# A scan followed by a mixture of adapters: stores of four chunks, ScalarE copies as words, and a new static order

## The chip, the cores and the metric

The kernel runs on one core of one Trainium2 chip. The metric is the device time of one execution in microseconds (us), the median of several runs; lower is better.

## What is computed

```
a, b: (8, 6400, 128) float32
h = 0;  for t in range(6400):  h = a[:, t] * h + b[:, t];  x[:, t] = h     # per batch and channel
x = x.reshape(51200, 128)
logits = x @ w_gate                         # (51200, 8)
w = softmax over the two largest logits of each row
delta = sum over the two chosen experts e of  w_e * ((x @ A[e]) @ B[e])   # rank 16
out = x + delta                             # (51200, 128) float32
```

The inputs a and b are 26.2 MB each and the output is 26.2 MB, so some 78.6 MB pass between HBM and the core.

## The kernel before

The 51,200 rows are cut into 100 **chunks** of 512 rows, and a chunk into four **blocks** of 128. Each step of a chunk is an operation with a name, and a table `ORDER` lists, for each of the five instruction queues (`pe` TensorE, `act` ScalarE, `dve` VectorE, `pool` GpSimd, `sp` SyncE), in which order that queue issues its operations. The table is fixed in the source. What an operation waits for is worked out from its dependences and turned into semaphore waits; a queue that waits holds everything behind it.

The steps, with their names in `ORDER` and their lines:

- `la`, `lb` (L396, SP): load a and b. From chunk 4 on one transfer brings two chunks (512 KB) in rows of 4 KB; the first four chunks come singly in rows of 2 KB. There are `NL` = 6 buffers each for a and b, and a load waits until TensorE has read the pair that was in its buffer six pairs earlier.
- `A`, `B`, `P` (L417, TensorE): turn a and b to channels by rows in PSUM, by transposes. `P17` holds b of chunk 17 and a of chunk 18.
- `ae` (L435, ScalarE): copy a from PSUM to SBUF. `fi` (L446, TensorE): `FILL` transposes of the identity matrix into pA ahead of chunks 7 to 14, whose results are not used.
- `sc` (L482, VectorE): the scan along the rows, into xT, float16, a ring of `NX` chunks.
- `Z` (L500, TensorE): logits and x @ A for a unit of mostly six blocks; `ze` (L506, ScalarE) copies them to zl, a ring of `NZ` blocks.
- `g1` to `g8`, `gx` (L534 to L554, VectorE and GpSimd) and `w1` (L549, ScalarE): the gate weights of a group of units, mostly 24 blocks.
- `mu` (L569, GpSimd or VectorE): multiply by the gate weights into zw.
- `T` (L578, TensorE): transpose zw into PSUM, float16. `te` (L300, ScalarE or VectorE): copy it to zwT in SBUF.
- `D` (L588, L589, TensorE): x by the identity plus zwT @ B. `oe` (L300, ScalarE or VectorE): copy the result to outt, a ring of `NO` blocks.
- `st` (L631, SP): store one entry of `STORES`, in chunks. With two chunks each partition holds eight rows of the output side by side, so the transfer has rows of 4 KB; with one chunk, 2 KB.

Which row of the output lies in which partition follows from the store that a chunk belongs to (`tile_of`). `xblock` picks the rows of a block with that stride, so the logits of any block of a store wait for the scans of all its chunks (`zlogits`, `fronts`). `SPLIT` sends the store of chunk 68 as two transfers of 124 and 4 partitions. The last twelve chunks (`TAIL_CHUNKS`) also use the PSUM banks of pA and pB for their results.

Which engine does `te`, `oe`, `mu` and most gating steps follows from the list of `ORDER` in which the name stands.

Of the kernel before, what the change touches and what calls it, by code (L numbers as in the profile page):

```python
# [12 lines left out]
STORES = [2] * 48 + [1] * 4  # L13
SPLIT = {68: [124, 4]}
TOP8 = 4
WARM = 16
FILL = {k: 4 for k in range(7, 15)}
# [3 lines left out]
NX = 24  # L21
NZ = 120
NO = 72
NW = 4
NG = 8
NS = 16
TAIL_CHUNKS = 12
ORDER = {
# [16 lines left out]
    ),  # L45
    "act": (
# [16 lines left out]
    ),  # L63
    "dve": (
# [14 lines left out]
    ),  # L79
    "pool": (  # L80
# [8 lines left out]
    ),  # L89
# [641 lines left out]
```

## Time and profile before

| What | Value |
|---|---|
| Median of 3 runs | 201.59 us (201.13 to 202.28) |
| Profiled execution | 201.01 us, span 199.2 us |
| TensorE, ScalarE, VectorE, GpSimd busy | 93%, 89%, 88%, 68% of the span |
| Mean rate of the DMA engines | 398 GB/s, 22,921 packets |
| Granted TensorE clock | 0.994 |
| Stores | 53 transfers: 47 of 512 KB, 4 of 256 KB, one of 496 KB and one of 16 KB |

The span runs from the first to the last instruction of the profiled execution; the rest of its time lies around it. A share of busy time is a mean over the whole span, with filling and emptying in it. A DMA share in the views adds up the recorded times of packets on 16 engines; packets of one engine overlap a little in the records, so a full stretch shows slightly over 1.

### The profile page before, as it was taken

The page shows a single profiled execution, that of the slowest core. Times are in us where ns is not written, and L with a number is a line of the kernel's source. Part 1 is how long each engine was busy: PE and PEld are TensorE (multiplying, and loading weights), DVE is VectorE, ACT ScalarE, POOL GpSimd, SP SyncE. Part 2 cuts the span into 40 slices and gives each one's busy share as a digit, 9 for nine tenths or more (in the row PEclk, how much of TensorE's full clock was granted, in tenths as well). Part 3 has the DMA queues.
Part 4 walks back from the last instruction along what each step waited for, and adds up shares of the span by engine and source line. Part 5 has one row for each costly group of instructions (what it writes and reads, how often), then busy time and mean ns, then how long its engine had stood idle before and what let it go on. Part 6 is the DMA issues. An engine that isn't in the chain of part 4 may idle for free.

```text
span 199.2 us, 7709 instructions
## 1 busy us (share of the span) xinstructions
PE 185.2 (93%) x3224; PEld 165.5 (83%) x3224; DVE 175.0 (88%) x291; ACT 176.9 (89%) x327; POOL 136.0 (68%) x168
## 2 busy tenths in 40 slices
PE   6899999999998979999999999999999999999990
PEld 6778888889987968899989989889988978878970
DVE  1599999989999879799999999999999899899980
ACT  2378699999988979899999999999999989999981
POOL 3210186878786657969989998796598978676520
PEclk9999999999999999999999999999999999999997
DMA  5999999999999999999999999999999999999796
GB/s 214 385 414 406 410 407 407 409 406 410 411 410 413 414 411 412 415 414 408 414 415 406 411 410 416 411 411 415 414 412 414 417 410 412 406 393 392 298 405 254
DMA packets 22921, 79.26 MB, mean 398 GB/s; under 512 B 2664, under 2 KB 2920, under 8 KB 22888
## 3 DMA queue, kind: packets, MB, share of 16 engines
q1 hardware_dynamic: 22312, 78.39, 98.1%
q8 instruction: 25, 0.41, 0.8%
q10 hardware_dynamic: 576, 0.40, 0.6%
q14 instruction: 8, 0.07, 0.1%
HBM read 52.56 MB, written 26.21 MB: 395 GB/s over the span
## 4 chain that ended last, share of the span: by engine, by line
PE 80%; ACT 5%; DMA 4%; issue 3%; SPq 2%; POOL 2%; DVE 1%; DVEq 0%
PE pB L417 23%; PE pO L588 13%; PE pZ L500 13%; PE pO L578 12%; PE pO L589 10%; PE pA L417 5%; DMA a_tm<-in_a_dram 4%; ACT outt L300 3%; PE pA L446 2%; SPq L396 2%; POOL zw L569 2%; ACT zwT L300 1%; ACT a_st L435 1%; ACT zl L506 1%; DVE xT L482 1%
## 5 line engine op out<-in xcount | busy, mean ns | idle before, releaser
L482 DVE TENSOR_TENSOR_SCAN xT<-a_st,xT,pB 128x512 f16<-128x512 f32 x96 | 120.4, 1254 | 6.6 <-PE pA L417 3.1
L569 POOL TENSOR_TENSOR zw<-zl,g 128x512 f16<-128x512 f32 x90 | 94.5, 1065 | 29.2 <-DVE g L554 23.2
L417 PE MATMUL pB<-ident_f,b_tm 64*128 64x64 f32 (+1 forms) x784 | 67.5, 229 | 1.2 <-issue 0.5
L417 PE MATMUL pA<-ident_f,a_tm 64*128 64x64 f32 (+1 forms) x784 | 67.8, 229 | 0.6 <-issue 0.4
L435 ACT COPY a_st<-pA 128x512 f32<-128x512 f32 x100 | 59.0, 613 | 7.9 <-PE pA L417 7.2
L417 PEld LDWEIGHTS pB<-ident_f,b_tm 64*128 64x128 f32 (+1 forms) x784 | 55.8, 139 | 10.9 <-issue 3.4
L506 ACT COPY zl<-pZ 128x816 f32<-128x816 f32 (+1 forms) x69 | 58.1, 842 | 1.7 <-PE pZ L500 1.6
L588 PE MATMUL pO<-ident_h,xT 128*128 128x128 f16 x368 | 55.2, 233 | 2.0 <-issue 1.8
L417 PEld LDWEIGHTS pA<-ident_f,a_tm 64*128 64x128 f32 (+1 forms) x784 | 56.0, 139 | 1.2 <-DMA a_tm<-in_a_dram 0.7
L300 ACT COPY outt<-pO 128x512 f32<-128x512 f32 x87 | 52.2, 609 | 4.6 <-PE pO L589 4.1
L589 PE MATMUL pO<-cst_h,zwT 128*128 128x128 f16 x368 | 53.0, 219 | 1.7 <-issue 1.7
L588 PEld LDWEIGHTS pO<-ident_h,xT 128*128 128x128 f16 x368 | 46.3, 144 | 4.9 <-issue 2.1
L589 PEld LDWEIGHTS pO<-cst_h,zwT 128*128 128x128 f16 x368 | 39.6, 108 | 1.8 <-issue 1.8
L500 PE MATMUL pZ<-cst_h,xT 128*128 128x136 f16 x400 | 37.8, 229 | 0.5 <-issue 0.4
L578 PE MATMUL pO<-ident_h,zw 128*128 128x128 f16 x368 | 35.5, 220 | 1.1 <-POOL zw L569 0.4
L500 PEld LDWEIGHTS pZ<-cst_h,xT 128*128 128x128 f16 x400 | 30.6, 145 | 1.5 <-DVE cst_h L324 0.2
L578 PEld LDWEIGHTS pO<-ident_h,zw 128*128 128x128 f16 x368 | 22.3, 97 | 5.5 <-POOL zw L569 1.3
L300 DVE COPY zwT<-pO 128x512 f16<-128x512 f16 x56 | 23.0, 414 | 3.5 <-PE pO L578 3.1
L300 ACT COPY zwT<-pO 128x512 f16<-128x512 f16 x36 | 21.4, 600 | 0.9 <-PE pO L578 0.8
L545 POOL TENSOR_TENSOR L<-L,k 128x192 f32<-128x192 f32 x14 | 8.8, 631 | 4.6 <-DVE L L543 4.0
L482 DVE TENSOR_TENSOR_SCAN xT<-a_st,pB 128x512 f16<-128x512 f32 (+1 forms) x8 | 7.5, 938 | 4.5 <-PE pB L417 4.4
L548 POOL TENSOR_TENSOR k<-k,L 128x192 f32<-128x192 f32 (+1 forms) x17 | 9.1, 535 | 2.5 <-DVE L L539 1.8
(56 smaller groups left out, 120.0 us busy)
## 6 DMA issues: line engine op xcount, KB each, us to landing
a_tm<-in_a_dram SPq DMA_DIRECT2D x48, 512.0 KB, 13.3
b_tm<-in_b_dram SPq DMA_DIRECT2D x48, 512.0 KB, 13.4
out_dram<-outt SPq DMA_DIRECT2D x47, 512.0 KB, 11.9
a_tm<-in_a_dram SPq DMA_DIRECT2D x4, 256.0 KB, 4.9
out_dram<-outt SPq DMA_DIRECT2D x4, 256.0 KB, 4.0
b_tm<-in_b_dram SPq DMA_DIRECT2D x3, 256.0 KB, 5.6
out_dram<-outt SPq DMA_DIRECT2D x1, 496.0 KB
b_tm<-in_b_dram ACTq DMA_DIRECT2D x1, 256.0 KB, 4.0
```

Of the source, the lines that this page charges most:

```text
L300: return e.copy(dst, src) if e is eng["act"] else e.tensor_copy(dst, src)
L417: last = e.transpose(*args)
L435: lambda e: e.copy(a_st[c % NA][:, :], pA[:, c % 2, :]))
L482: last = e.tensor_tensor_scan(out=x[:, s0:s1], data0=a_st[c % NA][:, s0:s1], data1=pB[:, c % 2, s0:s1], initial=init, op0=ALU.mult, op1=AL ...
L500: last = e.matmul(pZ[:, k // (n // 2), o : o + W], xblock(b0 + k), Awg_h)
L506: lambda e: e.copy(zl[:, zb : zb + n, :].rearrange("p (h k) w -> p h (k w)", h=2), pZ[:, :, 0 : n // 2 * W]))
L545: d3 = wide(5, [d3], lambda e: e.tensor_tensor(out=ll, in0=ll, in1=kk, op=ALU.add))
L548: d6 = wide(7, [d2, d5], lambda e: e.tensor_tensor(out=kk, in0=kk, in1=ll, op=ALU.add))
L569: lambda e: e.tensor_tensor(out=wv, in0=zv, in1=gv, op=ALU.mult))
L578: last = e.transpose(ptile[:, k * 128 : k * 128 + 128], zz[:, k, :], ident_h[:, :])
L588: e.matmul(dst, xblock(b0 + k), ident_h[:, :], start=True, stop=False)
L589: last = e.matmul(dst, zt[:, k * 128 : k * 128 + 128], B_h, start=False, stop=True)
```

## The change

- `STORES`: 22 stores of four chunks, four of two and four of one, where there were 48 of two and four of one. With four chunks a partition holds sixteen rows of the output side by side, so such a transfer has 1 MB in rows of 8 KB.
- `te` on ScalarE: the same bytes are copied as 256 float32 words instead of 512 float16 elements. On VectorE it stays as it was.
- `FILL`: two transposes instead of four ahead of each of the chunks 7 to 14.
- Rings: xT from 24 to 32 chunks, outt from 72 to 96 blocks, zl from 120 to 80 blocks.
- `ORDER`: all five lists are new, and with them the engine of some operations. ScalarE has 68 `te` and 83 `oe` (before 38 and 95), VectorE 32 `te`, 17 `oe` and 13 `mu` (before 62, 5 and 10).
- `AHEAD`, `TREE` and `MASK` are added with values for which they do nothing: an added dependence between operations of SP that lie 1000 apart (the list has 133), and another form of the last gating step for the groups in `MASK`, which is empty.

```diff
-STORES = [2] * 48 + [1] * 4
-SPLIT = {68: [124, 4]}
+STORES = [2,2]+[4]*16+[2,2]+[4]*6+[1]*4
+SPLIT = {68:[124,4]}
...
-FILL = {k: 4 for k in range(7, 15)}
+FILL = {k:2 for k in range(7,15)}
...
-NX = 24
-NZ = 120
-NO = 72
+NX = 32
+NZ = 80
+NO = 96
...
+AHEAD = 1000
+TREE = ()
+MASK = ()
...
+        for before, op in zip(self.order["sp"], self.order["sp"][AHEAD:]):
+            op.deps = op.deps + [before]
...
-            o_te[c] = P.add("dve act", f"te{c}", J, [o_T[c]] + get(o_D, c - NW),
-                            lambda e: copy(e, zt, ptile[:, 0:C]))
+            o_te[c] = P.add("dve act", f"te{c}", J // 2, [o_T[c]] + get(o_D, c - NW),
+                            lambda e: e.copy(zt.bitcast(F32), bank[:, 0 : C // 2]) if e is eng["act"]
+                            else e.tensor_copy(zt, ptile[:, 0:C]))
```

The lists of SP from the last loads on, before and after:

```diff
-la96 st58 lb96 st60 la98 st62 st72 st64 lb98 st66 st68 st78 st76 st70 st74 st82 st80 st86 st84 st90 st88 st92 st94 st96 st97 st98 st99
+la96 lb96 la98 st56 st60 lb98 st68 st70 st64 st72 st76 st80 st84 st88 st92 st96 st97 st99 st98
```

More of the change, by code (lines that the diff above doesn't have):

```diff
@@ L552, in gating @@
                     zlast[zpos[u] + k] = d5 if top else d2
-            o_g[gi] = wide(8, [a1, d5] + (get(o_mu, glast[gi - NG]) if gi >= NG else []),
-                           lambda e: e.scalar_tensor_tensor(
-                               out=gg, in0=ll, scalar=0.0, in1=sg, op0=ALU.is_ge, op1=ALU.mult))
+            free = get(o_mu, glast[gi - NG]) if gi >= NG else []
+            if gi in MASK:
+                d8 = wide(9, [d5, d6], lambda e: e.tensor_scalar(
+                    out=ll, in0=ll, scalar1=0.0, scalar2=1.0, op0=ALU.is_ge, op1=ALU.mult))
+                o_g[gi] = P.add("pool dve", f"gf_{gi}", nb, [a1, d8] + free,
+                                lambda e: e.tensor_tensor(out=gg, in0=ll, in1=sg, op=ALU.mult))
+            else:
+                o_g[gi] = wide(8, [a1, d5] + free, lambda e: e.scalar_tensor_tensor(
+                    out=gg, in0=ll, scalar=0.0, in1=sg, op0=ALU.is_ge, op1=ALU.mult))
         def back(gi, c):
```

121 rows, old and new, of the table ORDER are left out of this document.

## The prediction

> **What bounds the kernel now.** I read the page first: the five engines' shares, then the forty slices, then the DMA queues.
>
> ```profile
> span 199.2 us, 7709 instructions
> ...
> PE 185.2 (93%) x3224; PEld 165.5 (83%) x3224; DVE 175.0 (88%) x291; ACT 176.9 (89%) x327; POOL 136.0 (68%) x168
> ...
> DMA  5999999999999999999999999999999999999796
> GB/s 214 385 414 406 410 407 407 409 406 410 411 410 413 414 411 412 415 414 408 414 415 406 411 410 416 411 411 415 414 412 414 417 410 412 406 393 392 298 405 254
> ...
> q1 hardware_dynamic: 22312, 78.39, 98.1%
> q8 instruction: 25, 0.41, 0.8%
> ```
>
> Four engines stand near 90%, so the shares alone name no bound. The slices do: the DMA engines move 406 to 417 GB/s from the third slice to the thirty-fourth, flat, whatever the engines do. The profiled execution took 201.01 us with this span of 199.2, so 1.8 us lie around the span; the median of the runs, 201.59 us, is 0.58 above it.
>
> The windows view tests this. Its columns are busy time of PE, PEld, DVE, ACT, POOL (with instructions), granted clock, DMA share, GB/s.
>
> ```profile
> 70.00:80.00 10.00, 8.25 (x151) 7.29 (x148) 8.45 (x13) 8.60 (x17) 6.57 (x9) 1.00 1.02 411
> 100.00:110.00 10.00, 10.00 (x196) 9.26 (x197) 9.82 (x15) 9.98 (x19) 9.15 (x12) 1.00 1.03 412
> 175.00:185.00 10.00, 9.80 (x155) 8.42 (x152) 9.91 (x27) 9.70 (x21) 6.39 (x8) 1.00 0.98 390
> 185.00:195.00 10.00, 8.90 (x136) 7.80 (x133) 8.10 (x37) 9.14 (x21) 3.54 (x5) 1.00 0.90 357
> 195.00:199.20 4.20, 0.00 (x0) 0.00 (x0) 0.00 (x0) 0.00 (x0) 0.00 (x0) 0.73 0.60 230
> ```
>
> PE falls to 8.25 of 10 in one stretch and is full in another, and the DMA rate is 411 and 412. So the bytes set the pace until about 175 us; only in the last 24 us does the share drop, to 0.98, 0.90 and 0.60, where 1.03 is full. The chain of waits gives PE 80%, but PE is followed there through its own queue; how long a transfer waits tells more. The DMA view for 30 to 160 us (columns: count, size, median us from issue to landing), and the queue's own waits:
>
> ```profile
> DMA packets 14631, 53.56 MB, mean 412 GB/s; under 512 B 1620, under 2 KB 1620, under 8 KB 14606
> ...
> b_tm<-in_b_dram SPq DMA_DIRECT2D x38, 512.0 KB, 13.6
> a_tm<-in_a_dram SPq DMA_DIRECT2D x37, 512.0 KB, 13.7
> out_dram<-outt SPq DMA_DIRECT2D x32, 512.0 KB, 14.7
> ```
>
> ```profile
> SPq L396 <- PE pA L417: 36.1, 26, 4.3
> SPq L631 <- ACT outt L300: 23.3, 13, 5.0
> ...
> SPq L631 <- ACT sd L549: 12.9, 4, 8.8
> ```
>
> A load lands 13.6 us after its issue, while 512 KB at 412 GB/s take 1.27 us: ten or eleven transfers stand in line. SP does wait for free buffers (36.1 us in 26 waits, 4.3 at most) and for outputs (8.8 at most), but each wait is shorter than the line, so it never runs empty. A faster engine alone buys nothing here; fewer or cheaper packets do.
>
> **The change part by part.**
>
> *Rows of 8 KB.* 22 stores of four chunks replace 44 of two: 22 x 1 MB in 8 KB rows are 2816 packets where 5632 of 4 KB were, and 52 stores become 30. Bytes stay. What a packet costs beside its bytes is read from packets of two sizes. Stretches of 2 KB rows are the last stores, the head's loads, and a wider stretch of the head that has 4 KB rows and tiny constants in it:
>
> ```profile
> DMA packets 316, 0.59 MB, mean 391 GB/s; under 512 B 32, under 2 KB 32, under 8 KB 316
> ...
> q1 hardware_dynamic: 316, 0.59, 102.2%
> ```
>
> ```profile
> DMA packets 216, 0.40 MB, mean 395 GB/s; under 512 B 26, under 2 KB 26, under 8 KB 216
> ```
>
> ```profile
> 5.00:10.00 5.00, 4.50 (x37) 3.84 (x36) 2.62 (x3) 1.78 (x4) 1.10 (x1) 1.00 1.05 384
> ```
>
> The first is 195.5 to 197 us (single-chunk stores), the second 7 to 8 us. At 391 GB/s over 16 engines a 2 KB packet takes 16 x 2048 / 391 = 83.8 ns, at 412 a 4 KB packet 159.1 ns. Two kilobytes more cost 75.3 ns, so 8.5 ns belong to the packet, its part of the completion write included (8 data packets and one such write per engine and transfer at either size, and with 8 KB rows still). An 8 KB packet then takes 309.7 ns where two of 4 KB take 318.2: 2816 x 8.5 / 16 = 1,496 ns, **1.5 us**. With 395 the packet's part is 6.8 ns and the gain 1.2 us; with 384, 11.6 ns and 2.0 us. I take 391 because those are stores, and alone on the queue.
>
> The other bound lies above nothing: the 16 KB packets of queue 8 took 0.8% of 16 x 199.2 us, 25.5 us for 25, or 1.02 us each, 62 ns per KB where 4 KB packets take 39. [...] For the range I let this term lie between 0 and -2.0 us; a loss as large as queue 8's rate (510 ns per 8 KB, +34 us) I leave out, because the length would then come from size alone, and from 2 to 4 KB the cost per byte falls.
>
> [...]
>
> *The copies of zwT.* On ScalarE a copy of 512 f16 elements becomes one of 256 f32 words.
>
> ```profile
> L300 ACT COPY zwT<-pO 128x512 f16<-128x512 f16 x36 | 21.4, 600 | 0.9 <-PE pO L578 0.8
> L300 ACT COPY outt<-pO 128x512 f32<-128x512 f32 x87 | 52.2, 609 | 4.6 <-PE pO L589 4.1
> L357 ACT CAST cst_h<-pZ 128x128 f16<-128x128 f32 x1 | 0.3, 265 | 0.3 <-PE pZ L351 0.3
> L300 DVE COPY zwT<-pO 128x512 f16<-128x512 f16 x56 | 23.0, 414 | 3.5 <-PE pO L578 3.1
> L300 DVE COPY outt<-pO 128x512 f32<-128x512 f32 x5 | 3.4, 674 | 0.5 <-PE pO L589 0.5
> L569 DVE TENSOR_TENSOR zw<-zl,g 128x512 f16<-128x512 f32 x10 | 6.8, 684 | 0.0
> ```
>
> f16 and f32 of one count take the same 600 and 609 ns, so elements count. Between 128 elements (265) and 512 (609), 256 give about 380 ns. The new order has 68 such copies on ScalarE (38 before) and 83 output copies (95 before): 68 x 0.38 - 38 x 0.60 - 12 x 0.609 = -4.3 us. VectorE gives up 30 copies of zwT, takes 12 output copies and three multiplications: -30 x 0.414 + 12 x 0.674 + 3 x 0.684 = -2.3 us, and five more gating steps of some 0.25 us take back about one. GpSimd loses what these take over. Under the full line that is worth 0 until 175 us. It counts after: behind the copy of chunk 98's a, ScalarE has 11 output copies and 10 of zwT where it had 18 and 7, that is 11 x 0.609 + 10 x 0.38 = 10.5 us for 15.2.
>
> *Fillers.* Sixteen transposes go, at 0.11 us each by the chain's rows:
>
> ```profile
> 16.82 0.44 PE pA L446 x4
> ```
>
> That is 1.8 us of PE between 14 and 26 us. Loads queue there too, so I cost it at nothing; if that cover were missing it would gain, at most 1.8.
>
> *Places and orders.* A block of a four-chunk tile needs all four scans before its logits, two chunks (3.8 us at 1.9 us a chunk) later than now. Cover: the new order of PE runs the transposes of the loads 21 chunks ahead of those of zw around chunk 49, for 18 before; xT has 32 chunks for 24 and outt 24 for 18, but zl only 80 blocks for 120. A store of four waits for four output copies, and the loads behind it on SP wait as well: that is the rival below. Before the last load of b, 64 chunks are stored instead of 68, so 36 are left for the end, not 32. This and ScalarE's 4.7 us give the last stretch more to send: in 185 to 195 the share of 0.90 leaves (1.03 - 0.90) / 1.03 x 10 = 1.3 us unused. I take **0.5 us** of it, the range being 0 to 1.3, because the last stores still wait for the last chunks' scans, gating and copies.
>
> Sum: 199.2 - 1.5 - 0.5 = 197.2 span, 199.0 for the profiled execution, and with the 0.58 above it **199.6 us** as median, 1.0% less. What this kernel's measurement can tell from no change is about 0.5%, 1.0 us.
>
> **The rivals.**
>
> *The rows bring little* (0.13). Rows of 8 KB may go out as packets of 4 KB, or the cost per packet may grow with the row, and the end stays bound by the last chunks. The four-chunk order then trades equal things: 201.6 with nothing saved, 201.0 with half of the 1.2 us; both within 0.5%. For it: no 8 KB packet of queue 1 in the trace. Against it: the cost per packet in two stretches, 6.8 and 8.5 ns. [...]
>
> *SP's line runs dry* (0.19, the slower side). A store of four at SP's head waits for its fourth output copy, and no load behind it goes out. The longest such wait is 8.8 us; doubled, as four chunks double it, it is 17.6 us, against 13.6 us of line. The DMA engines then stand for 4.0 us per such wait. One of them: 201.59 - 1.5 + 4.0 = 204.1; two short ones of 2 us the same. It decides from the point where a store's wait exceeds 13.6 us, in the stretch from 30 us on. For it: the stores' waits in the two rows above come to 36 us already (23.3 + 12.9). Against it: only 4 of those 17 waits are behind gating, the longest of the others is 5.0 us, and stores of 1 MB also lengthen the line.
>
> *More than the sum* (0.06). The dearer packet (2.0 us) and the full 1.3 us of the end: 201.59 - 3.3 = 198.3; with the fillers' 1.8 it would be 196.5.
>
> **How the numbers follow.** The forecast has 0.62; its own range is 198.6 to 200.5. Faster by over 0.5%: 0.62 + 0.06 = 0.68, less 0.01 for its edge, 0.67. Same: 0.13 and that edge, 0.14. Slower: 0.19. The range goes from 198.0, past the third rival's middle, to 202.9, which takes in the second rival where the line is dry for under 2.8 us; left out are the rest of that (0.1) and the far end of the third and others (some 0.08).
>
> **What would show it.** In the new profile the DMA view should have about 2,800 fewer packets of 4 KB and 30 stores, 22 of 1024 KB; between 30 and 160 us the rate should rise from 412 to about 416 GB/s (a third of the bytes at 423), with the share still 1.02 to 1.03. ScalarE's zwT copy should read 128x256 f32 and about 380 ns. The last two windows should show more than 0.90 and 0.60. It is wrong if the rate stays at 412, or if slices in the middle show DMA below 9 and SP's waits at the store line reach 13 us.

## The result and the profile after

The changed kernel takes 203.7 us (median of 4 runs, 202.82 to 204.59) where the kernel before takes 201.49 (median of 4, one more than the three behind the 201.59 above): a ratio of 1.0114, 95% interval 1.0082 to 1.0145. It is 1.1% slower. The forecast was 199.6 us and faster, the range ended at 202.9.

The profiled execution took 204.59 us, the longest of the four. Its page, in the lines that answer to those shown of before:

```profile
span 202.8 us, 7647 instructions
...
PE 188.6 (93%) x3208; PEld 166.8 (82%) x3208; DVE 175.8 (87%) x282; ACT 173.2 (85%) x345; POOL 127.7 (63%) x159
...
GB/s 217 371 419 409 406 406 408 399 383 415 380 414 402 362 415 415 414 356 376 356 417 410 398 422 409 417 407 415 409 417 408 420 415 423 417 409 388 280 346 288
DMA packets 19753, 79.26 MB, mean 391 GB/s; under 512 B 2312, under 2 KB 2568, under 8 KB 16904
...
L593 ACT COPY zwT<-pO 128x256 f32<-128x256 f32 x62 | 23.6, 392 | 3.4 <-PE pO L588 2.3
```

Everything that the change set out to make smaller is smaller. There are 3,168 fewer packets: the 2,816 of the forecast, and 22 fewer transfers with 16 packets under 512 B each (2,312 of these on the page, 2,664 before). In the trace the 2,816 packets of 8 KB take 309 ns each (median; estimate 309.7), those of 4 KB 159 and those of 2 KB 84. The copy of zwT takes 392 ns (estimate 380, before 600). ScalarE is busy 3.7 us less. The span is 3.6 us longer all the same. What is new in the slices is their middle: before, the rate was flat; now it falls to 362, 356 and 376. The windows view of the changed kernel (columns as in the prediction) shows where:

```profile
90.00:100.00 10.00, 9.56 (x186) 8.69 (x184) 9.02 (x12) 9.51 (x20) 8.46 (x11) 1.00 0.98 345
150.00:175.00 25.00, 24.87 (x452) 22.15 (x451) 22.83 (x33) 23.04 (x48) 20.59 (x25) 1.00 1.02 416
175.00:185.00 10.00, 9.72 (x144) 8.25 (x143) 9.52 (x27) 9.29 (x19) 6.53 (x8) 1.00 1.00 412
185.00:195.00 10.00, 9.60 (x156) 8.69 (x153) 9.75 (x34) 9.61 (x28) 5.64 (x8) 1.00 0.71 293
```

Where the transfers run undisturbed (150 to 175 us) the rate is 416 GB/s, the figure that was forecast for 30 to 160 us. From 90 to 100 us it is 345 with a share of 0.98: by their records the DMA engines hardly stood, their packets took longer (those of 4 KB 185 ns in the mean, 162 in the kernel before), and no run shows why. In the last full stretch the share is 0.71, where it was 0.90 before and more than that was forecast, while TensorE is busy for 9.60 of 10 us (8.90 before), VectorE for 9.75 (8.10) and ScalarE for 9.61 (9.14). So at the end it is the computation that is late. The DMA view from 30 to 160 us, and the waits of SP's queue over the whole span:

```profile
DMA packets 12566, 52.18 MB, mean 401 GB/s; under 512 B 1391, under 2 KB 1391, under 8 KB 11039
...
out_dram<-outt SPq DMA_DIRECT2D x15, 1024.0 KB, 16.1
```

```profile
SPq L400 <- PE pA L421: 63.7, 33, 7.2
...
SPq L642 <- ACT outt L304: 18.0, 9, 4.9
...
SPq L642 <- ACT sd L553: 5.6, 1, 5.6
```

The mean rate is 401, not the 416 forecast. The waits at the store line are 5.6 us at most. What grew is the wait of loads for free buffers, 63.7 us in 33 waits where it was 36.1 in 26: the loads wait for TensorE to have read. TensorE's lag is there already after 30 us. The same window of the kernel before and of the changed kernel, and the first scan in each:

```profile
0.00:30.00 30.00, 27.42 (x366) 23.68 (x366) 22.22 (x37) 19.27 (x35) 8.70 (x18) 1.00 0.95 372
...
6.60 1.22 DVE L482 TENSOR_TENSOR_SCAN xT<-a_st,pB 128x512 f16<-128x512 f32 x1 [4.39 <-PE pB L417]
```

```profile
0.00:30.00 30.00, 25.91 (x318) 21.86 (x320) 20.04 (x33) 16.80 (x32) 8.04 (x18) 1.00 0.96 371
...
9.92 1.22 DVE L486 TENSOR_TENSOR_SCAN xT<-a_st,pB 128x512 f16<-128x512 f32 x1 [7.72 <-ACT a_st L439]
```

By 30 us TensorE has begun 48 multiplications fewer, 16 of them fillers, and the first scan starts 3.3 us later.

### The profile page after: what moved, and what is told of

Same layout as the page of the kernel before. It is cut to its first block, busy times and chain, and to the rows that moved or that the text cites. A ratio compares the mean times of both kernels' runs of the same rounds, so it can differ in the third digit from the quotient of the medians.

```text
span 202.8 us, 7647 instructions
## 1 busy us (share of the span) xinstructions
PE 188.6 (93%) x3208; PEld 166.8 (82%) x3208; DVE 175.8 (87%) x282; ACT 173.2 (85%) x345; POOL 127.7 (63%) x159
## 2 busy tenths in 40 slices
DMA packets 19753, 79.26 MB, mean 391 GB/s; under 512 B 2312, under 2 KB 2568, under 8 KB 16904
## 4 chain that ended last, share of the span: by engine, by line
PE 64%; DVE 17%; ACT 6%; POOL 4%; issue 4%; DMA 2%; SPq 0%; DVEq 0%; POOLq 0%
PE pB L421 20%; PE pZ L504 11%; PE pO L599 10%; DVE xT L486 10%; PE pO L588 9%; PE pO L600 7%; PE pA L421 5%; POOL zw L579 4%; DVE zw L579 3%; DMA a_tm<-in_a_dram 2%; ACT zl L510 2%; ACT outt L304 2%; ACT a_st L439 2%; DVE g L564 1%; ACT zwT L593 1%
## 5 line engine op out<-in xcount | busy, mean ns | idle before, releaser
L579 POOL TENSOR_TENSOR zw<-zl,g 128x512 f16<-128x512 f32 x87 | 90.8, 1063 | 22.5 <-DVE g L564 18.1
L421 PE MATMUL pA<-ident_f,a_tm 64*128 64x64 f32 (+1 forms) x784 | 70.2, 231 | 2.1 <-issue 1.3
L421 PE MATMUL pB<-ident_f,b_tm 64*128 64x64 f32 (+1 forms) x784 | 69.9, 231 | 1.9 <-DVE cst_h L328 0.6
L421 PEld LDWEIGHTS pB<-ident_f,b_tm 64*128 64x128 f32 (+1 forms) x784 | 57.1, 140 | 11.9 <-issue 4.4
L304 ACT COPY outt<-pO 128x512 f32<-128x512 f32 x76 | 45.3, 607 | 4.3 <-PE pO L600 3.0
L588 PE MATMUL pO<-ident_h,zw 128*128 128x128 f16 x368 | 34.2, 220 | 1.2 <-issue 0.5
L593 ACT COPY zwT<-pO 128x256 f32<-128x256 f32 x62 | 23.6, 392 | 3.4 <-PE pO L588 2.3
L552 POOL TENSOR_TENSOR k<-k,L 128x192 f32<-128x192 f32 (+2 forms) x16 | 8.6, 535 | 17.1 <-DVE k L542 11.0
L594 DVE COPY zwT<-pO 128x512 f16<-128x512 f16 x30 | 12.3, 411 | 2.7 <-PE pO L588 2.5
L304 DVE COPY outt<-pO 128x512 f32<-128x512 f32 x16 | 10.9, 680 | 1.3 <-PE pO L600 1.2
```

The costliest lines, as they stand in the source:

```text
L304: return e.copy(dst, src) if e is eng["act"] else e.tensor_copy(dst, src)
L421: last = e.transpose(*args)
L579: lambda e: e.tensor_tensor(out=wv, in0=zv, in1=gv, op=ALU.mult))
L588: last = e.transpose(ptile[:, k * 128 : k * 128 + 128], zz[:, k, :], ident_h[:, :])
L593: lambda e: e.copy(zt.bitcast(F32), bank[:, 0 : C // 2]) if e is eng["act"]
L594: else e.tensor_copy(zt, ptile[:, 0:C]))
```

## The experiments

All ratios are to the kernel before, with the 95% interval; the changed kernel itself stands at 1.0114.

**Is the row size worth anything? (rows of 4 KB in the changed kernel)**

```diff
+                if m == 4:
+                    return [e.dma_start(dst[:, h : h + 8], view[:, h : h + 8]) for h in (0, 8)]
...
-                       sem=dma_sem(f"st{len(o_st) % NS}"), parts=len(cuts))
+                       sem=dma_sem(f"st{len(o_st) % NS}"), parts=2 if m == 4 else len(cuts))
```

> The changed kernel, but each store of four chunks goes out as two transfers of 4 KB rows at the same place of the order; nothing else differs. Theory O (the 8 KB rows gain about 1.5 us as predicted, and the new order loses more than that in the middle and at the end): slower than the changed kernel by 0.5 to 1.5 us, 204.2 to 205.2 us. Rival R (8 KB rows or transfers of 1 MB are themselves what costs): faster than the changed kernel, back towards 201.5 us.

Measured: 1.0132 (1.0074 to 1.019). The intervals lie over each other: the 8 KB rows are worth no time that can be measured here, and rival R's return towards 201.5 us did not come. From 150 to 175 us, where the changed kernel has 416 GB/s, this one has 414:

```profile
150.00:175.00 25.00, 24.84 (x451) 22.13 (x448) 22.80 (x33) 22.99 (x49) 20.57 (x25) 1.00 1.03 414
```

**Is the sagging middle the loss? (stores of chunks 8 to 28 moved on SP)**

```diff
-la40 lb40 lb44 la42 la46 lb42 la44 lb48 st8 lb46 la48 st12 la50 la52 lb50 lb52 la54 lb54 la56 lb56 lb58 lb60 la60 la58 la62 lb62 lb64 st20 st16 la64 st24 la66 la68 lb66 lb68 la70 st28
+la40 lb40 st8 lb44 la42 la46 lb42 la44 st12 lb48 lb46 la48 la50 la52 st16 lb50 lb52 la54 lb54 la56 lb56 st20 lb58 st24 lb60 la60 la58 la62 lb62 st28 lb64 la64 la66 la68 lb66 lb68 la70
```

> The changed kernel, but on SP the stores of chunks 8, 12, 16, 20, 24 and 28 stand where the profile shows their outputs ready (the store of chunk 16 was ready at 72.4 us and issued at 97.2), ahead of loads that wait for buffers. Theory O with the loss in the middle (SP's line runs dry because ready stores stand behind waiting loads): the rate between 30 and 160 us rises from 401 to at least 410 GB/s and the time falls by 1 to 3 us, 200.7 to 202.7. Rival E (the end alone decides, since the last chunks are computed too late): the rate rises, the time stays within 0.5 us of 203.7. Rival R: neither changes.

Measured: 1.0201 (1.0145 to 1.0257). The DMA view from 30 to 160 us, a wait of TensorE's weight loads between 100 and 110 us, and two windows right behind it:

```profile
DMA packets 12788, 53.27 MB, mean 410 GB/s; under 512 B 1414, under 2 KB 1414, under 8 KB 11194
```

```profile
PEld pB L421 <- DMA a_tm<-in_a_dram: 3.0, 1, 3.0
```

```profile
104.00:106.00 2.00, 1.24 (x24) 1.24 (x26) 0.08 (x1) 0.08 (x1) 1.55 (x2) 0.55 1.03 424
106.00:108.00 2.00, 2.00 (x30) 1.78 (x30) 1.89 (x3) 1.59 (x4) 0.00 (x0) 0.59 1.01 414
```

The rate rose from 401 to 410, and the time with it, which none of the theories had: the stores now stand ahead of loads on SP, TensorE stood 3.0 us for one load, and behind that its granted clock was 0.55 and 0.59 for some 4 us. A higher DMA rate in the middle does not by itself bring the end forward. Whether the sagging rate costs the changed kernel time stays open, as the moved stores brought this stall with them.

**Is it the last chunks? (chunks 98 and 99 ahead of the backlog)**

```diff
-... Z64 T82 T83 D82 D83 Z65 T84 B99 T85 D84 D85 T86 P98 T87 D86 D87 T91 Z66 T90 T88 T89 D91 Z67 ...
+... Z64 P98 B99 T82 T83 D82 D83 Z65 T84 Z66 T85 D84 D85 T86 Z67 T87 D86 D87 T91 Z68 T90 T88 T89 D91 ...
```

(with the scans and copies of these chunks moved up on VectorE and ScalarE)

> The changed kernel with the last chunks' steps moved ahead of the backlog: on TensorE the transposes of chunk 98's b and 99's a, then of 99's b, right behind the logits of unit 64 (they stood at 184.8 us, 6.0 us after the load of b landed), the logits of units 66 to 68 further up, and the copies, scans and unit copies that belong to them likewise. Theory T: 1 to 4 us faster, 199.7 to 202.7. Rival H: within 0.6 us of 203.7, since the same backlog is only worked off later. Nothing else differs.

Measured: 1.0278 (1.0228 to 1.0328), slower than the changed kernel by some 3 us, where theory T said 1 to 4 us faster and rival H no difference. The theory of the tail fell in this form. That what is moved ahead holds back what it passes is a likely reason, not a shown one.

**Words and fillers alone (kernel before)**

```diff
-FILL = {k: 4 for k in range(7, 15)}
+FILL = {k: 2 for k in range(7, 15)}
...
-                            lambda e: copy(e, zt, ptile[:, 0:C]))
+                            lambda e: e.copy(zt.bitcast(F32), bank[:, 0 : C // 2]) if e is eng["act"]
+                            else e.tensor_copy(zt, ptile[:, 0:C]))
```

> The kernel before with ScalarE's copies of zwT as words and fillers of two instead of four; orders and stores as before. Theory O: within 0.7 us of the kernel before, 200.8 to 202.2, as nothing of it lies on the transfers' path. Rival W (fewer fillers or the word copies slow the head or TensorE): 202.5 us or more.

Measured: 0.9986 (0.9952 to 1.002). Each copy on ScalarE falls from 600 to 384 ns, ScalarE is busy 171.7 us instead of 176.9, and the time stays, as theory O had it.

**Four-chunk stores alone (kernel before)**

```diff
-STORES = [2] * 48 + [1] * 4
+STORES = [2, 2] + [4] * 16 + [2, 2] + [4] * 6 + [1] * 4
...
-NZ = 120
-NO = 72
+NZ = 96
+NO = 96
```

(and the five orders of before, shifted only as far as the wait for four scans asks)

> The kernel before with the stores of the change (22 of four chunks, 8 KB rows) and outt of 96 and zl of 96 blocks; its own orders, in which an operation moves only as far as the wait for four scans asks (some logits by 0.8 to 2.6 us), and each store of four at the place of the later of its two halves. Theory O: the rows gain what was predicted, 0.5 to 1.5 us, so 200.0 to 201.0 us. Rival R: slower than the kernel before by 1 to 3 us, 202.5 to 204.5.

Measured: 1.0655 (1.0599 to 1.0712), 215.25 us, far outside both forecasts. Waits between 30 and 170 us, and a window:

```profile
ACT zl L505 <- PE pZ L499: 11.0, 17, 1.3
DVE zwT L299 <- PE pO L577: 6.3, 13, 1.1
...
PEld pZ L499 <- DVE xT L481: 4.1, 10, 1.1
PEld pZ L499 <- ACT zl L505: 4.0, 8, 1.1
```

```profile
180.00:185.00 5.00, 4.59 (x89) 3.94 (x87) 3.74 (x6) 4.24 (x10) 3.14 (x3) 1.00 0.35 138
```

The logits now wait for scans (`PEld pZ <- DVE xT`), their copies for the logits; in the same stretch of the kernel before the waits of PEld for these do not occur, and that of ScalarE is this:

```profile
ACT zl L506 <- PE pZ L500: 0.4, 1, 0.4
```

At 180 us the DMA engines are a third busy: the backlog of compute ends the kernel.

**The rings as a control (kernel before)**

```diff
-NZ = 120
-NO = 72
+NZ = 96
+NO = 96
```

> The kernel before with zl of 96 and outt of 96 blocks (120 and 72), all else as it was: the control for the rings in the run with stores of four on the orders of before. Theory G (the wait for four scans made that run 14 us slower): within 1 us of 201.5. Rival Z (the smaller ring of zl did): 4 us slower or more.

Measured: 1.0001 (0.9982 to 1.0021). These rings cost nothing. The change's own rings (zl of 80 blocks, xT of 32 chunks) were not run apart.

**Four-chunk stores without the wait for four scans (kernel before)**

```diff
+            def xpair(b):
+                c = b // J
+                s0, n = (c // 2 * 2, 2) if c < NCH - 4 else (c, 1)
...
-            c1 = sum(tile_of[(b0 + n - 1) // J]) - 1
+            c1 = (b0 + n - 1) // J
+            c1 = c1 | 1 if c1 < NCH - 4 else c1
...
-                    last = e.matmul(pZ[:, k // (n // 2), o : o + W], xblock(b0 + k), Awg_h)
+                    last = e.matmul(pZ[:, k // (n // 2), o : o + W], xpair(b0 + k), Awg_h)
...
-            o_D[c] = P.add("pe", f"D{c}", J, [o_te[c]], delta)
+            o_D[c] = P.add("pe", f"D{c}", J, [o_te[c], o_sc[sum(tile_of[c]) - 1]], delta)
```

(with the stores, the rings and the list of SP of the run with four-chunk stores; the last step `D` still waits for all four scans)

> The orders of before, rings of 96 and 96 blocks, stores of four chunks in 8 KB rows, but the logits take their rows as if the store were a pair, and so wait for two scans instead of four (the gate weights and zw then belong to other rows: that part of the computation is changed). Theory G (the wait for four scans is what the stores of four cost): 200 to 202.5 us, near the kernel before, for 215.3 with the wait. Rival S (transfers of 1 MB, sent when the fourth chunk is done, cost by themselves): 208 us or more.

Measured: 1.0038 (1.0013 to 1.0062), 202.12 us. The wait of the logits' copies is back at that of before, in the same stretch:

```profile
ACT zl L512 <- PE pZ L506: 0.4, 1, 0.4
```

So of the 13.8 us between 201.43 and 215.25, 13.1 belong to the wait for four scans and the shifted orders that it asks for. The stores of 1 MB in rows of 8 KB, without that wait, cost 0.7 us and gain nothing.

**Undo the grouping on the new orders (changed kernel, pairs at the places of the fours)**

```diff
-STORES = [2,2]+[4]*16+[2,2]+[4]*6+[1]*4
+STORES = [2] * 48 + [1] * 4
...
-st20 st16 la64 st24
+st20 st22 st16 st18 la64 st24 st26
```

> The changed kernel with stores of two chunks as before (48 pairs and four singles, 4 KB rows), each former store of four as two pairs at its place; its orders and rings otherwise as they are, so that logits wait for two scans again where four were asked. Theory G (the wait for four scans costs in the changed orders): 1 to 3 us faster, 200.7 to 202.7. Rival Q (the orders on the engines cost, wherever the waits are): within 0.7 us of 203.7, as each engine still issues in the same order.

Measured: 1.0187 (1.0143 to 1.0231), if anything slower than the changed kernel, so neither forecast came. Taking the grouping away does not win the time back. That the price now lies in the orders that were drawn for it fits this, but no run shows it by itself.

**What bounds the kernel before? Transfers, TensorE, both ways**

Less to transfer (stores of chunks 8 to 27 write 16 of 128 partitions, some 11 us of transfers), in the kernel before:

```diff
-            cuts = SPLIT.get(c, [128])
+            cuts = [16] if 8 <= c < 28 else SPLIT.get(c, [128])
```

> The kernel before with the same 20 chunks' stores cut to 16 of 128 partitions (that part of the output is left out). If the transfers bound the kernel before, as the prediction has it: 3 to 10 us faster than 201.5, as the loads come earlier until computation becomes the bound. If computation bounds the kernel before as well (theory C for both): within 1 us of 201.5.

The same in the changed kernel:

> The changed kernel, but the stores of chunks 8 to 27 write only 16 of the 128 partitions (that part of the output is left out), so 4.6 MB or about 11 us of transfers go in the middle. Theory C (computation in the order bounds the changed kernel): within 1.5 us of 203.7. Rival D (the transfers still bound it): 6 us or more faster, below 197.7.

Measured: 0.9948 (0.9921 to 0.9974) before, 1.0051 (1.0024 to 1.0078) changed. In both, 11 us less to send bring 0.5% to 0.6%, one microsecond: theory C's number, in both kernels.

Less for TensorE (chunks 40 to 63 without zwT @ B, 96 multiplications), in the kernel before and in the changed one:

```diff
-                    e.matmul(dst, xblock(b0 + k), ident_h[:, :], start=True, stop=False)
+                    last = e.matmul(dst, xblock(b0 + k), ident_h[:, :], start=True, stop=40 <= c < 64)
+                    if 40 <= c < 64:
+                        continue
```

> The kernel before without the product of zwT and B in chunks 40 to 63 (that part of the output is left out): 96 matmuls, some 5.8 us of TensorE's stream less. Theory P: 2 to 5.8 us faster, until the transfers become the bound. Rival D: within 1 us of 201.5.

> The changed kernel with the same 96 matmuls left out. Theory P: 2 to 5.8 us faster than 203.7; and where the transfers then bound both, this kernel gains more than the one before, as its rows of 8 KB need 1.5 us less of them. Rival D: within 1 us of 203.7.

Measured: 0.9969 (0.9939 to 0.9998) before, 1.0211 (1.0178 to 1.0245) changed, where less work even went with a longer time, which neither theory had. The relief is smaller than was expected: TensorE's busy time falls by 2.3 us in the kernel before (185.2 to 182.9) and by 2.1 in the changed one (188.6 to 186.5), not by 5.8. More for TensorE in the kernel before (two identity transposes ahead of each of the chunks 40 to 63, 48 x 0.11 = 5.3 us):

```diff
-FILL = {k: 4 for k in range(7, 15)}
+FILL = {k: 4 for k in range(7, 15)} | {k: 2 for k in range(40, 64)}
```

(with `fi40` to `fi63` ahead of these chunks' transposes in the list of TensorE)

> The kernel before with two more transposes of the identity ahead of each of the chunks 40 to 63 (results unused), 48 in all, 5.3 us of TensorE's stream at 0.11 us each. Theory P (TensorE's stream, in its fixed order, is the bound: what is added to it or idles in it comes out at the end): 3.5 to 6 us slower than 201.5, 205.0 to 207.5. Rival D (the transfers bound the kernel before, and TensorE has room beside them): within 1 us of 201.5.

Measured: 1.0152 (1.0126 to 1.0178), +3.0 us, between the two forecasts and nearer to theory P's. TensorE's busy time grew by 5.9 us (185.2 to 191.1).

**All reliefs at once**: fewer bytes, less TensorE and the copies as words, in the kernel before, and the first two reliefs in the changed kernel, which has the words. The edits are the diffs shown above, together, with `FILL` left at four in the kernel before.

> The kernel before with three reliefs at once: the stores of chunks 8 to 27 write only 16 of 128 partitions and the product of zwT and B is left out in chunks 40 to 63 (both parts of the output are left out), and ScalarE copies zwT as words. Each alone moved the time by less than 1 us. Theory N (transfers, TensorE and ScalarE each stand within a microsecond of the bound, so that only all of them together move the end): 2 to 6 us faster than 201.5, 195.5 to 199.5. Rival F (something else, scans or the last chunks, holds the time): within 1.5 us of 201.5.

> The changed kernel with the same reliefs (it copies words already). Theory S (the changed orders hold the time by their waits, on no engine's own work): within 2 us of 203.7. Rival N (the engines' work bounds it as in the kernel before): 2 to 6 us faster, 197.7 to 201.7.

Measured: 0.9786 (0.9752 to 0.9819) before, 197.37 us; 1.0135 (1.008 to 1.0189) changed. In the kernel before the single reliefs brought 0.52%, 0.31% and 0.14%, 0.97% in sum, and together 2.14% (theory N). In the changed kernel they bring nothing (theory S). The 0.14% had the shorter fillers in it, and no two of the three were tried without the third. The window 60 to 90 us of the kernel before, and of it with all reliefs:

```profile
60.00:90.00 30.00, 27.49 (x510) 24.75 (x508) 26.22 (x40) 27.04 (x51) 21.64 (x26) 1.00 1.03 413
```

```profile
60.00:90.00 30.00, 27.82 (x524) 25.29 (x522) 27.05 (x41) 27.03 (x53) 22.45 (x27) 1.00 0.91 354
```

The DMA share goes from 1.03 to 0.91 and the engines do hardly more in that time (524 multiplications begun for 510): full transfer engines aren't all that holds them.

**Is it the head?** The change also swaps the first loads: SP has `la1 la0 la2 lb1` for `la0 lb1 la1`, ScalarE `ae1 ae0` for `ae0 ae1`. First the changed kernel with chunk 0 ahead again:

```diff
-la1 la0 la2
+la0 la1 la2
...
-ae1 ae0
+ae0 ae1
```

> The changed kernel with two places of the head put back: the load of chunk 0's a ahead of chunk 1's on SP, and the copy of chunk 0's a ahead of chunk 1's on ScalarE (the first scan started at 9.9 us, at 6.6 before). Theory H (the compute engines, TensorE first, bound the changed kernel from the head on, so that work lost there is never made up): 0.8 to 2.5 us faster than 203.7, 201.2 to 202.9. Rival T (the order of the last chunks alone): within 0.6 us of 203.7.

Measured: 1.0084 (1.0048 to 1.0119); its first scan starts at 6.77 us. That is 0.3% less than the changed kernel, and the intervals overlap: no more than rival T's number, though the theory of the tail behind it had fallen. Then the reverse, the new head alone in the kernel before, and the old head in the changed kernel with the joint reliefs:

```diff
-la0 lb1 la1
+la1 la0 lb1
...
-ae0 ae1
+ae1 ae0
```

> The kernel before with the head of the change alone: SP loads a of chunk 1 ahead of a of chunk 0 and b of chunk 1, ScalarE copies a of chunk 1 ahead of that of chunk 0. The first scan should start at 8 to 10.5 us instead of 6.6. Theory H (the head makes what is left of the loss): the kernel before has no slack in front, so the 1.5 to 3.9 us of delay come out at the end, ratio 1.007 to 1.019. Theory O (the orders between 30 and 175 us make it, and the head's delay is made up in the stream of transfers): 1.000 to 1.004.

> The changed kernel with the joint relief (stores of chunks 8 to 27 write 16 of 128 partitions, no product of zwT with B in chunks 40 to 63) and, new, the head of the kernel before (a of chunk 0 loaded and copied ahead of chunk 1). Without the head the relief left 1.0135. Theory H (a late head is the delay that no relief further on can touch): the relief now comes through, 0.980 to 0.998. Theory O (the orders' own waits further on hold it): 1.005 to 1.013, the head worth the 0.3% that it was worth without relief.

Measured: 1.0085 (1.0047 to 1.0124) for the head alone in the kernel before, and 1.0099 (1.0071 to 1.0128) for the relieved changed kernel with the old head. So the head by itself can cost the kernel before most of what the whole change costs, theory H's number; but taking it out of the changed kernel leaves the other delay, theory O's number, relieved or not. The profiled execution with the new head took 204.75 us, near the longest of its twelve (201.92 to 204.8), so its trace shows a dear case. The timeline of TensorE in the kernel before, and with the new head (start, length, operation, and in brackets the idle time before it):

```profile
1.67 2.82 PE L321 MATMUL pO<-ident_f 128*128 128x128 f32 x12 [1.67 <-POOL ident_f L305]
4.28 1.06 PE L417 MATMUL pA<-ident_f,a_tm 128*128 128x128 f32 x4
...
5.89 0.60 PE L417 MATMUL pB<-ident_f,b_tm 128*128 128x128 f32 x4
6.32 0.60 PE L417 MATMUL pA<-ident_f,a_tm 128*128 128x128 f32 x4
```

```profile
5.11 1.11 PE L417 MATMUL pA<-ident_f,a_tm 128*128 128x128 f32 x4 [0.62 <-DMA a_tm<-in_a_dram]
...
6.88 1.06 PE L417 MATMUL pB<-ident_f,b_tm 128*128 128x128 f32 x4
7.73 1.06 PE L417 MATMUL pA<-ident_f,a_tm 128*128 128x128 f32 x4
8.58 1.06 PE L417 MATMUL pB<-ident_f,b_tm 128*128 128x128 f32 x4
```

Chunk 0's a is loaded second and comes 0.62 us late. That alone would be small; but four transposes then go on taking 1.06 us up to 9.4 us at least, where in the kernel before they take 0.60 to 0.66 from 5.9 us on. ScalarE waits for chunk 1's a before it copies chunk 0's, and the first scan starts at 9.93 us instead of 6.60.

## Why the prediction was wrong

**The bound: the step that failed first.** "A faster engine alone buys nothing here; fewer or cheaper packets do." The first half held (words: nothing; less TensorE: 0.3%). The second did not follow from it: 11 us of transfers left out brought one microsecond. A DMA share of 1.03 from 30 to 160 us shows that the DMA engines were full, not that they alone set the pace. The joint relief shows what the pace depends on: transfers, TensorE and ScalarE together bring 2.14% where each alone brings at most 0.52%, so each single relief stops at another bound within about a microsecond (which two of the three go together was not tried), while half or more of what was added to TensorE is paid (3.0 us of 5.3 to 5.9). The row that was quoted to test this, PE at 8.25 of 10 and the DMA rate unchanged, spoke of one stretch of 10 us, and slack there is no slack over the run.

**Rows of 8 KB.** Their size was right: the packet count, 309 ns for a packet of 8 KB where 309.7 was worked out, and 416 GB/s where nothing disturbs (414 there with 4 KB rows on the same orders). Their worth, -1.5 us, was not: 4 KB rows on the same orders are no slower within the intervals, and on the orders of before four-chunk stores cost 0.7 us even without their wait. The rival "the rows bring little" was right on this part; its cause, packets that stay at 4 KB or cost more, was not.

**Words and fillers.** Right: 392 ns for 380, ScalarE 3.7 us less for 4.3 (the whole change), and no gain before 175 us. VectorE, set at some 1.3 us less, is busy 0.8 us more (175.0 to 175.8). What was hoped for after 175 us did not come: in the kernel before, words and shorter fillers left the time as it was, and in the changed kernel all three engines were late there.

**Places and orders.** Set at -0.5 us (0 to -1.3), this term had the wrong sign, and its range did not allow for a loss. The wait for all four scans was named and costed at nothing, with 21 chunks of lead as its cover. On the old orders it costs 13 us, with the shifts that it asks for. With the redrawn orders 203.7 us are measured for 215.25, so all but about 2 us of that is gone. And the part of the orders that was never costed is their first entries: the swapped loads, worth 0.85% alone in the kernel before. The 4.7 us that ScalarE was to have less "behind the copy of chunk 98's a" were misread too: that copy stands later in the new list, so fewer copies are left behind it. From chunk 82 on, ScalarE has 15 output copies and 13 of zwT where it had 18 and 7, by the same prices 14.1 us for 15.2. The copy in the kernel before, and in the changed one:

```profile
176.69 0.65 ACT L435 COPY a_st<-pA 128x512 f32<-128x512 f32 x1
```

```profile
185.34 0.60 ACT L439 COPY a_st<-pA 128x512 f32<-128x512 f32 x1
```

**The slower rival** had the sign and, by accident, nearly the time (204.1). Its mechanism did not occur: no store at the head of SP's line waited 13 us, the longest 5.6, and where the line was thin (loads issued from 90 to 100 us land after 6.4 to 7.7 us, where 13.6 was usual) the loads had waited for buffers.

**What stays open.** The loss of the changed kernel has at least two parts of about the same size that don't add: the head, and something further on that stands when the head is repaired (1.0084) and when bytes and TensorE work are taken away as well (1.0099). Moving the stores in the middle or the steps of the last chunks, or undoing the grouping, did not win it back. The traces show where the second part arises. With the old head the changed kernel has begun 357 multiplications by 30 us, the kernel before with words and as few fillers 356; from 30 to 160 us it begins 52 fewer, with TensorE no less busy (first the kernel before, then the changed one with the old head):

```profile
30.00:160.00 130.00, 123.80 (x2327) 112.52 (x2324) 120.83 (x170) 120.90 (x227) 105.43 (x126) 1.00 1.03 412
```

```profile
30.00:160.00 130.00, 124.92 (x2275) 111.78 (x2276) 119.52 (x165) 119.61 (x234) 96.05 (x114) 1.00 1.01 406
```

Over the whole span the same 3,208 multiplications keep TensorE busy for 183.1 and for 187.5 us, so in the new order TensorE takes longer for the same work. Whether that comes from the new sequence of its steps or from waits too short to be listed, no run shows. The waits that relief leaves untouched are candidates as well, for instance GpSimd's for the gate weights between 30 and 175 us, in the changed kernel and in it with both reliefs:

```profile
POOL zw L579 <- DVE g L564: 13.5, 9, 5.7
```

```profile
POOL zw L579 <- DVE g L564: 13.3, 9, 5.6
```

```profile
POOL zw L569 <- DVE g L554: 15.3, 14, 2.9
```

The third is the kernel before: more waits, but none over 2.9 us. No run has shown that they hold the end. No version beat the kernel before without leaving work out.

## What to carry to other kernels

A resource at 100% is the bound only once relief of it alone has moved the end; where several are within a microsecond of each other, a change that helps one brings little (here 0.52% at most), and a change that delays one can cost a good part of the delay (here 3.0 us of 5.3 to 5.9). Before a transfer is made larger, look at which computations its grouping ties together: on the old orders the wait for four scans cost nearly twenty times what the transfer's size did. When orders are drawn anew, read their first ten entries as closely as the part that the change is about.

## What the hardware showed

A short pause at the start went with a delay longer than the pause. In the kernel before, TensorE is busy without a break from 1.67 us, and four transposes fall from 1.06 to 0.60 us at about 5.9 us, 4.2 us later (from start to start 0.85 and 0.43 us). With the new head in it, a pause of 0.62 us ends at 5.11 us, and they stay at 1.06 up to 9.4, at least 4.3 us more. The granted clock reads 1.00 over the first 30 us of both, so only the durations show it. It doesn't always come: the timeline of the changed kernel with both reliefs has a pause of 0.45 us, and from the second group behind it on the transposes take 0.60 us.

```profile
4.80 1.02 PE L421 MATMUL pA<-ident_f,a_tm 128*128 128x128 f32 x4 [0.45 <-DMA a_tm<-in_a_dram]
5.66 0.60 PE L325 MATMUL pO<-ident_f 128*128 128x128 f32 x4
```

There the first scan starts at 8.28 us. By an estimate from the three starts, 6.60, 8.28 and 9.93 us, about half of the 3.3 us of delay comes from the swapped order and half from the slow transposes. Of the nine traces with the new head, seven have the first scan between 9.78 and 10.53 us and two at 8.28 and 8.36. In the run with moved stores the granted clock itself fell, to 0.55 and 0.59 between 104 and 108 us, behind TensorE's stand of 3.0 us. What decides whether the transposes stay slow behind a pause, no run shows.
